# Small tiles padded so that the operands behind them start at multiples of 128 bytes of a partition

## The chip, the core and the metric

The kernel runs on one core of one Trainium2 chip. The metric is the device time of one execution in microseconds (us). Five engines work side by side and are tied by semaphores: TensorE (PE in the profile, its weight loads as PEld), VectorE (DVE), ScalarE (ACT), GpSimd (POOL) and SyncE (SP), which issues the transfers.

## What is computed

A gated linear-attention layer with a running state (mLSTM) for 4 batches, 8 heads, 768 steps and head size 40, followed by a feed-forward layer whose nonlinearity is a quotient of polynomials. `q`, `k`, `v` and the gates come in as 32-bit floats, `w_in` and `w_out` as 64-bit ones, which the kernel splits into a high and a low part.

```python
for t in range(S):                                   # attention, per batch and head
    m_new = max(f[t] + m, i[t])
    C = exp(f[t] + m - m_new) * C + exp(i[t] - m_new) * outer(v[t], k[t]);  m = m_new
    n = (same decay) * n + (same gate) * k[t]
    y[t] = sigmoid(o[t]) * (C @ q[t]) / max(|n . q[t]|, 1)
x = y as [3072 tokens, 320]
h = x @ w_in                                         # [3072, 2048]
g = (a0 + a1 h + a2 h^2 + a3 h^3) / (1 + |b0||h| + |b1|h^2 + 1e-6)
out = g @ w_out                                      # [3072, 320]
```

## The kernel before

The tokens are worked in 12 blocks of 256. A block belongs to two attention units (`attention(u)`, 24 of them: six chunks of 128 steps times four batches), whose outputs are put together by `outputs(m)` and turned into a tile `xk` of [128, 5, 256] that holds x and its remainder in single-precision operands that TensorE reads at its fast rate (`F32R`). `feed_forward(n, i)` then runs eight times per block, each time over 256 of the 2048 inner features:

- `f_f1` makes `ph` (PSUM): 16 matmuls of 256 columns. The moving operand is a slice of `xk`, the stationary one 128 columns of `wi`, `wj` or `wY` (the weights and their remainders).
- ACT, DVE and POOL make g from `ph`, as a high part `gH` and a low part `gL`.
- `f_f2` adds to `po` (PSUM): 12 matmuls of 320 columns. Here the stationary operand is a slice of `gH` or `gL`, and the moving one is `wo`.

So there are 12 x 8 x 16 = 1536 matmuls into `ph` and 12 x 8 x 12 = 1152 into `po`, all `F32R`. The attention's matmuls and transposes (`ps`, `ow`, `y`, `kq`, `px`) are plain `F32`. A plain `F32` product of two operands appears in the profile as two matmuls, a transpose (`kq`, `px`) as one. `hot` are matmuls of `ident` with `ident` that keep TensorE busy while the first inputs arrive.

The order of the instructions on every engine is a list of names written out in the file (`ORDER`); the place of each tile follows from the pools, which lay their tiles one behind the other and begin each at a multiple of 32 bytes of the partition. The pool `common` comes first, with `ident`, `cd` (two numbers), `kp`, `qn0`, `vb0` and `g`; then the constants with the states `st0` to `st5` and `sm0`, `sm1`, the weights, and the working pools with `tm`, `na`, `xk`, `ha`, `w`, `p`, `gH`, `gL` and `ot`. Since `cd` takes 32 bytes and a state 672, nearly everything behind them starts 32, 64 or 96 bytes past a multiple of 128.

```python
c = {name: pool.tile(shape, F32, name=name) for name, shape in (
    ("ident", [P, P]), ("cd", [P, 2]), ("kp", [P, H, L]), ...
st = [cp.tile([DP, NP, E1], F32, name=f"st{j}") for j in range(B + 2)]
```

Of the kernel before, what the change touches and what calls it, by code (L numbers as in the profile page):

```python
# [10 lines left out]
F32 = mybir.dt.float32  # L11
# [298 lines left out]
def kernel(tc: tile.TileContext, *args):  # L310


    with ExitStack() as ctx:
        common = _prologue(ctx, tc, args)
        flag = common.pop("flag")()
        with tc.If(flag > 0) as test:
            _program(tc, True, common, *args)
        with test.Else():
            _program(tc, False, common, *args)


def _prologue(ctx, tc, args):


    nc = tc.nc
    P, L, H, D, BH = 128, 64, 8, 40, 32
    pool = ctx.enter_context(tc.tile_pool(name="common", bufs=1))
    c = {name: pool.tile(shape, F32, name=name) for name, shape in (
        ("ident", [P, P]), ("cd", [P, 2]), ("kp", [P, H, L]), ("qn0", [P, H, L]), ("vb0", [P, H, 2, D + 1]),
        ("g", [P, H * L]),  # L330
    )}
    c["flag"] = _can_square(ctx, tc, args[8])
    for j, src in enumerate((args[4], args[3])):
        nc.sync.dma_start(
            c["g"][0:BH, j * 4 * L : (j + 1) * 4 * L], src.rearrange("b h s -> (b h) s")[:, 0 : 4 * L]
        )
    nc.vector.memset(c["kp"], 0.0)
    nc.vector.memset(c["vb0"], 0.0)
    make_identity(nc, c["ident"])
    nc.gpsimd.memset(c["cd"][:, 0:1], CD)  # L340
    nc.gpsimd.memset(c["qn0"], 0.0)
    return c


def _can_square(ctx, tc, moe_a):

    pool = ctx.enter_context(tc.tile_pool(name="flag", bufs=1))
    a, b = (pool.tile([1, 4], F32, name=f"flag_{x}") for x in "ab")
    t = pool.tile([1, 4], F32, name="flag_t")
    out = pool.tile([1, 1], I32, name="flag_out")  # L350
    tc.nc.sync.dma_start(a, moe_a.unsqueeze(0))

    def decide():
        return _decide(tc, a, b, t, out)

    return decide


def _decide(tc, a, b, t, out):
    V = tc.nc.vector  # L360
    V.scalar_tensor_tensor(b, a, -1.0, a, op0=ALU.mult, op1=ALU.max)
    V.tensor_reduce(t[:, 0:1], b, axis=mybir.AxisListType.X, op=ALU.add)
    V.tensor_scalar(t[:, 1:2], b[:, 3:4], t[:, 0:1], 4.0, op0=ALU.mult, op1=ALU.mult)
    V.scalar_tensor_tensor(t[:, 1:2], a[:, 2:3], a[:, 2:3], t[:, 1:2], op0=ALU.mult, op1=ALU.is_le)
    V.tensor_scalar(t[:, 2:3], t[:, 0:1], 2.0**-20, 1e-30, op0=ALU.mult, op1=ALU.max)
    V.scalar_tensor_tensor(t[:, 2:3], t[:, 2:3], b[:, 3:4], t[:, 1:2], op0=ALU.is_le, op1=ALU.mult)
    V.tensor_copy(out, t[:, 2:3])
    return tc.nc.values_load(out, min_val=0, max_val=1)
# [3 lines left out]
def _program(  # L372
# [17 lines left out]
    B, H, S, D = q.shape  # L390
    DM, DFF = w_in.shape
    P = 128
    L = 64
    NB = S // P
    BH = B * H
    NP = H // 2
    DP = D + L
    E1 = D + 1
# [15 lines left out]
    cp = ctx.enter_context(tc.tile_pool(name="const", bufs=1))  # L414
# [6 lines left out]
    ident, cd = common["ident"], common["cd"]  # L421
# [10 lines left out]
    qn = [common["qn0"], cp.tile([P, H, L], F32, name="qn1")]  # L432
    kp = common["kp"]
    qt = [cp.tile([DP, NP, 2, L], F32, name=f"qT{j}") for j in range(2)]
    vb = [common["vb0"], cp.tile([P, H, 2, E1], F32, name="vb1")]
    st = [cp.tile([DP, NP, E1], F32, name=f"st{j}") for j in range(B + 2)]
    sm = [cp.tile([DP, NP, E1], F32, name=f"sm{j}") for j in range(2)]

    wt = {}
    wY = wp.tile([P, DFF], F32R, name="wY")  # L440
# [1 line left out]
    def ring(pool, tag, shape, name, dt=F32, at=None):  # L442
        k = plan.slot[tag] if at is None else at
        return pool.tile(shape, dt, tag=f"{tag}{k}", name=name, bufs=1)
# [387 lines left out]
    def attention(u):  # L832
        n, b = divmod(u, B)
# [3 lines left out]
        d = units[u] = {}  # L837
# [137 lines left out]
                )  # L975

        def decay(c, src):
            d[c] = ap1.tile([DP, NP, E1], F32, tag=f"tm{c}", name=f"tm{u}_{c}")
            nc.gpsimd.tensor_tensor(
                d[c], src, d["ab"][0:DP, c, :, L - 1 : L].broadcast_to([DP, NP, E1]), op=ALU.mult,  # L980
            )
# [51 lines left out]
        if later:  # L1033
            add("d0", "POOL", 0.7, lambda: decay(0, st[old]), r=[*ST2, "ab"], w=["t0"], new=[("t0", ("tm0", 1))])
        add("ow", "PE", 0.85, f_ow, r=["pm.1", "pm.00", "pm.01", V], w=["ow"], new=new("ow"))
        add("u0", "DVE", 0.66, lambda: update(0, s), r=["t0"] if later else [], w=["ow", *SM])
        add("d1", "POOL", 0.74, lambda: decay(1, s), r=[*SM, "ab"], w=["t1"], new=[("t1", ("tm1", 1))])
        d["i1"] = [f"qA_{u}", *(x[1:] for x in SM), *((x[1:] for x in ST2) if later else ())]
        if u % 2:
# [3 lines left out]
    def outputs(m):  # L1043
        n, b = divmod(2 * m, B)
        pair = [units[2 * m + j] for j in range(2)]
        home, bank = pair[0]["home"], pair[0]["bank"]
        d = {}
# [14 lines left out]
        def ye(k):  # L1062
            return d[k][:, 0 : H * E1].rearrange("p (h c e) -> p h c e", h=4, c=2)
# [12 lines left out]

        def f_ab(k):
            if "na" not in d:
                d["na"] = ring(ap1, "na", [P, 2, H], f"na{m}")
            nc.scalar.activation(d["na"][:, k].rearrange("p (h c) -> p h c", h=4), ye(k)[:, :, :, D], AF.Abs)  # L1080

        def f_rc():
# [56 lines left out]
        na = f"na{m}"  # L1139
        for k in range(2):  # L1140
            add("ab", "ACT", 0.1, lambda k=k: f_ab(k), w=[f"y{k}at{m}", f"{na}.{k}"], new=[(na, ("na", 2))] if k == 0 else ())
# [235 lines left out]
    ap1 = ctx.enter_context(tc.tile_pool(name="att1", bufs=1))  # L1377
# [52 lines left out]
```

## Time and profile before

| | us |
|---|---|
| three runs | 514.69, 515.6, 521.54 (median 515.6) |
| the profiled execution | 514.69 |
| its span, first to last instruction | 512.9 |
| what lies around the span | 1.8 |

The profile shows busy time by engine, the clock that TensorE was granted, a chain of work followed back from the last instruction, and a timeline with the start of every instruction. Matmuls are pipelined: the duration of one is longer than the distance to the next, so what a matmul costs is read from the starts of a row of them, not from their durations.

### The profile page before, as it was taken

The numbers are of one execution on the slowest core, as the hardware profiler recorded it, in microseconds if no ns is written. First come the engines' busy times: TensorE is split into PE (matmuls) and PEld (weight loads), VectorE is DVE, ScalarE is ACT, GpSimd is POOL, SyncE is SP. The second block draws the span as 40 slices with busy tenths as digits, with TensorE's granted clock in tenths as the row PEclk, the third lists the DMA queues.
The fourth block names the chain that finished last, engine by engine and source line by source line (L and its number), as shares of the span: only waits on it lengthen the run. The fifth ranks groups of instructions, "written<-read, shape, count | busy, mean of one in ns | idle before, by whom it ended". The sixth has DMA issues, their size and how long they took to land.

```text
span 512.9 us, 14161 instructions
## 1 busy us (share of the span) xinstructions
PE 483.8 (94%) x5631; PEld 465.4 (91%) x5631; DVE 426.0 (83%) x702; ACT 402.4 (78%) x698; POOL 404.9 (79%) x375
## 2 busy tenths in 40 slices
PE   6898779999999999999999999999999999999991
PEld 6797679989999999999999999999999999999990
DVE  7889789889898988898797987877878787787890
ACT  1887788978798787788887789898778788869960
POOL 3679778989899988878787898868777889776770
PEclk9899899999999999999999999999999999999996
DMA  6998897415244341532422335311240120000001
GB/s 169 213 273 161 192 255 123 72 27 123 54 99 104 92 77 25 138 77 70 81 54 58 83 75 102 89 25 49 45 96 19 34 72 0 8 23 1 27 0 33
DMA packets 119117, 42.53 MB, mean 83 GB/s; under 512 B 103554, under 2 KB 111810, under 8 KB 119042
## 3 DMA queue, kind: packets, MB, share of 16 engines
q1 hardware_dynamic: 118912, 41.37, 37.0%
q8 instruction: 46, 0.75, 0.6%
q14 instruction: 29, 0.24, 0.2%
q10 hardware_dynamic: 130, 0.16, 0.1%
HBM read 36.90 MB, written 4.10 MB: 80 GB/s over the span
## 4 chain that ended last, share of the span: by engine, by line
PE 71%; DVE 9%; ACT 5%; DMA 4%; POOL 4%; issue 3%; SPq 1%; POOLq 0%; DVEq 0%; ACTq 0%
PE ph L34 29%; PE po L34 27%; PE y L34 4%; PE kq L34 3%; PE ow L34 3%; PE ps L34 2%; DMA rawo<-in_moe_w_out_dram 2%; DVE p L34 2%; POOL p L34 2%; DVE w L34 1%; PE px L34 1%; DMA rawi<-in_moe_w_in_dram 1%; DVE gL L34 1%; ACT ph L34 1%; DVE gH L34 1%
## 5 line engine op out<-in xcount | busy, mean ns | idle before, releaser
L34 POOL TENSOR_TENSOR p<-p,w 128x512 f32<-128x512 f32 (+1 forms) x97 | 129.5, 1335 | 56.4 <-DVE w L34 55.1
L34 PE MATMUL ph<-xk,wi 128*128 128x256 f32 x1152 | 167.5, 281 | 0.7 <-DVE pm L34 0.4
L34 PEld LDWEIGHTS ph<-xk,wi 128*128 128x128 f32 x1152 | 150.3, 188 | 1.8 <-ACT lo0i L34 0.6
L34 POOL TENSOR_TENSOR w<-w,ha 128x512 f32<-128x512 f32 (+1 forms) x97 | 129.9, 1343 | 10.7 <-ACT w L34 10.2
L34 PE MATMUL po<-wo,gH 128*128 128x320 f32 x768 | 135.5, 312 | 0.1
L34 PEld LDWEIGHTS po<-wo,gH 128*128 128x128 f32 x768 | 115.4, 188 | 1.3 <-DVE gH L34 0.3
L34 DVE SCALAR_TENSOR_TENSOR w<-w,gH 128x512 f32<-128x512 f32 (+1 forms) x97 | 89.5, 922 | 3.9
L34 ACT ACTIVATE ph<-w,cd 128x512 f32<-128x512 f32 (+1 forms) x97 | 66.5, 686 | 28.8 <-POOL w L34 14.4
L34 DVE SCALAR_TENSOR_TENSOR gL<-p,ps,ph 128x512 fp32r<-128x512 f32 (+1 forms) x97 | 71.0, 733 | 21.0 <-POOL p L34 20.0
L34 DVE SCALAR_TENSOR_TENSOR gH<-p,ps,ph 128x512 fp32r<-128x512 f32 (+1 forms) x97 | 71.2, 734 | 15.9 <-ACT ph L34 14.6
L34 PE MATMUL po<-wo,gL 128*128 128x320 f32 x384 | 79.8, 318 | 4.3 <-DVE gL L34 4.2
L34 ACT ACTIVATE w<-ha,ba 128x512 f32<-128x512 f32 (+1 forms) x97 | 78.4, 811 | 3.0
L34 DVE SCALAR_TENSOR_TENSOR p<-p,ps,ph 128x512 f32<-128x512 f32 (+1 forms) x97 | 70.6, 733 | 10.8 <-ACT p L34 10.6
L34 ACT ACTIVATE ha<-ph 128x512 f32<-128x512 f32 (+1 forms) x97 | 57.2, 592 | 24.4 <-PE ph L34 23.6
L34 ACT ACTIVATE p<-ph,ps 128x512 f32<-128x512 f32 (+1 forms) x97 | 65.5, 676 | 2.1 <-DVE gL L34 1.8
L34 PEld LDWEIGHTS po<-wo,gL 128*128 128x128 f32 x384 | 59.0, 188 | 7.5 <-DVE gL L34 6.5
L34 ACT ACTIVATE ph<-ph 128x512 f32<-128x512 f32 (+1 forms) x97 | 56.1, 579 | 2.1
L34 PE MATMUL ph<-xk,wY 128*128 128x256 f32 x192 | 53.5, 279 | 0.0
L34 PE MATMUL ph<-xk,wj 128*128 128x256 f32 x192 | 53.4, 278 | 0.0
L34 PEld LDWEIGHTS ph<-xk,wj 128*128 128x128 f32 x192 | 36.2, 188 | 0.0
L34 PEld LDWEIGHTS ph<-xk,wY 128*128 128x128 f32 x192 | 36.1, 188 | 0.0
L34 POOL TENSOR_TENSOR qA<-qT,ab 104x512 f32<-104x512 f32 x24 | 32.0, 1334 | 0.0
(128 smaller groups left out, 658.7 us busy)
## 6 DMA issues: line engine op xcount, KB each, us to landing
rawo<-in_moe_w_out_dram SPq DMA_DIRECT2D x8, 640.0 KB
ab<-scrA SPq DMA_DIRECT2D x40, 128.0 KB
rawi<-in_moe_w_in_dram SPq DMA_DIRECT2D x8, 512.0 KB
qn<-in_q_dram SPq DMA_DIRECT2D x24, 160.0 KB
kr<-in_k_dram SPq DMA_DIRECT2D x24, 160.0 KB
og<-in_o_gate_dram SPq DMA_DIRECT2D x48, 80.0 KB
vb<-in_v_dram SPq DMA_DIRECT2D x48, 80.0 KB
out_dram<-ot SPq DMA_DIRECT2D x23, 160.0 KB
```

The source lines that it names most:

```text
L34: made = fn(*args, **kwargs)
```

## The change

No instruction is added, taken away or moved: each engine has the same rows in the same order, 4785 of TensorE, 1468 of DVE, 1395 of ACT and 736 of POOL in the built program, and the same shapes (`padded` makes a longer tile and hands on a view of the old shape). Only the places of the tiles change. `cd` becomes 128 bytes long, `vb0` and `vb1` 2688 (2624 before), each state and decay product 768 (656 before, which took 672), and the normalisers `na` 128 (64 before).

```diff
-        ("ident", [P, P]), ("cd", [P, 2]), ("kp", [P, H, L]), ("qn0", [P, H, L]), ("vb0", [P, H, 2, D + 1]),
+        ("ident", [P, P]), ("cd", [P, 32]), ("kp", [P, H, L]), ("qn0", [P, H, L]), ("vb0", [P, 672]),
         ("g", [P, H * L]),
     )}
+    c["vb0"] = c["vb0"][:, 0 : H * 2 * (D + 1)].rearrange("p (h c e) -> p h c e", h=H, c=2)
...
-    vb = [common["vb0"], cp.tile([P, H, 2, E1], F32, name="vb1")]
-    st = [cp.tile([DP, NP, E1], F32, name=f"st{j}") for j in range(B + 2)]
-    sm = [cp.tile([DP, NP, E1], F32, name=f"sm{j}") for j in range(2)]
+
+    def padded(pool, shape, name, **kw):
+        n = int(np.prod(shape[1:]))
+        t = pool.tile([shape[0], -(-n // 32) * 32], F32, name=name, **kw)[:, 0:n]
+        names = "abc"[: len(shape) - 1]
+        return t.rearrange(f"p ({' '.join(names)}) -> p {' '.join(names)}", **dict(zip(names[1:], shape[2:])))
+
+    vb = [common["vb0"], padded(cp, [P, H, 2, E1], "vb1")]
+    st = [padded(cp, [DP, NP, E1], f"st{j}") for j in range(B + 2)]
+    sm = [padded(cp, [DP, NP, E1], f"sm{j}") for j in range(2)]
...
-            d[c] = ap1.tile([DP, NP, E1], F32, tag=f"tm{c}", name=f"tm{u}_{c}")
+            d[c] = padded(ap1, [DP, NP, E1], f"tm{u}_{c}", tag=f"tm{c}")
...
-                d["na"] = ring(ap1, "na", [P, 2, H], f"na{m}")
+                d["na"] = ring(ap1, "na", [P, 32], f"na{m}")[:, 0 : 2 * H].rearrange("p (k h) -> p k h", k=2)
```

Where the tiles lie, as the two built programs have it (bytes past a multiple of 128; all buffers of a name alike unless listed):

```
tile                              before             after
ident                             0                  0
kp, qn0, vb0                      32                 0
qn1, qT, vb1, ab                  96                 0
st0 .. st5                        32 64 96 0 32 64   0
wi, wj, wY, wo                    32                 0
pm, e, kT, qA, gt, kr             32                 0
xn, fb (its own buffer)           0                  0
g (also the other buffer of fb)   96                 0
xk                                96                 0
ha, w, p, gH, gL, ot              96                 0
pb, ps, ba (2 or 4 numbers each)  0 32 64            32 64 96
```

All slices that the matmuls take of `xk`, `wi`, `wj`, `wY`, `wo`, `gH` and `gL` begin whole multiples of 128 bytes into their tile.

## Rows read from the trace of the kernel before

**Rows 1.** The page: busy time by engine, and granted TensorE clock in 40 slices.

```profile
PE 483.8 (94%) x5631; PEld 465.4 (91%) x5631; DVE 426.0 (83%) x702; ACT 402.4 (78%) x698; POOL 404.9 (79%) x375
...
PEclk9899899999999999999999999999999999999996
```

**Rows 2.** The page: the chain that ended last, by engine and by line.

```profile
PE 71%; DVE 9%; ACT 5%; DMA 4%; POOL 4%; issue 3%; SPq 1%; POOLq 0%; DVEq 0%; ACTq 0%
PE ph L34 29%; PE po L34 27%; PE y L34 4%; PE kq L34 3%; PE ow L34 3%; PE ps L34 2%; DMA rawo<-in_moe_w_out_dram 2%; DVE p L34 2%; POOL p L34 2%; DVE w L34 1%; PE px L34 1%; DMA rawi<-in_moe_w_in_dram 1%; DVE gL L34 1%; ACT ph L34 1%; DVE gH L34 1%
```

**Rows 3.** Windows: busy PE, PEld, DVE, ACT, POOL; clock, DMA share, GB/s.

```profile
125.00:200.00 75.00, 74.87 (x938) 72.16 (x939) 66.37 (x101) 60.07 (x104) 67.70 (x62) 1.00 0.38 81
200.00:300.00 100.00, 99.95 (x1210) 96.86 (x1206) 85.64 (x131) 81.97 (x140) 82.85 (x76) 1.00 0.37 79
300.00:400.00 100.00, 99.79 (x1082) 97.70 (x1081) 82.17 (x127) 82.37 (x141) 80.22 (x73) 1.00 0.28 63
400.00:500.00 100.00, 99.06 (x1000) 96.91 (x999) 83.02 (x127) 82.24 (x144) 76.73 (x68) 1.00 0.06 17
```

**Rows 4.** Timeline of TensorE, 470 to 480 us: start, length, instruction, count.

```profile
473.02 1.33 PE L34 MATMUL po<-wo,gH 128*128 128x320 f32 x8
474.19 0.75 PE L34 MATMUL po<-wo,gL 128*128 128x320 f32 x4
474.77 1.33 PE L34 MATMUL po<-wo,gH 128*128 128x320 f32 x8
475.95 0.74 PE L34 MATMUL po<-wo,gL 128*128 128x320 f32 x4
476.53 0.87 PE L34 MATMUL ph<-xk,wi 128*128 128x256 f32 x6
477.24 0.28 PE L34 MATMUL ph<-xk,wj 128*128 128x256 f32 x1
477.35 0.28 PE L34 MATMUL ph<-xk,wY 128*128 128x256 f32 x1
...
478.26 0.28 PE L34 MATMUL ph<-xk,wY 128*128 128x256 f32 x1
```

**Rows 5.** Timeline of TensorE, 30 to 55 us: two rows of `hot`.

```profile
34.01 4.06 PE L34 MATMUL hot<-ident 128*128 128x128 f32 x34
...
38.72 1.60 PE L34 MATMUL hot<-ident 128*128 128x128 f32 x12
```

**Rows 6.** Timeline of TensorE, 458 to 460.5 us: the transposes of `xn`.

```profile
458.83 0.82 PE L34 MATMUL px<-ident,xn 128*128 128x128 f32 x6
```

**Rows 7.** Instructions on the tile `st`: duration in ns, least/median/most, then first and last start.

```profile
L34 PE MATMUL y<-st,qA x320: 227/227/248, 105.4 to 451.3; 40*64 40x41 f32 x160
L34 DVE TENSOR_TENSOR st<-tm,ow x24: 301/316/326, 34.5 to 456.6; 104x164 f32<-104x164 f32 x24
L34 POOL TENSOR_TENSOR tm<-st,ab x20: 455/467/1383, 76.8 to 449.1; 104x164 f32<-104x164 f32 x20
```

**Rows 8.** Instructions on the tile `ident`, in the same columns.

```profile
L34 PEld LDWEIGHTS hot<-ident x180: 186/192/338, 4.0 to 57.1; 128*128 128x128 f32 x180
...
L34 PEld LDWEIGHTS px<-ident,xn x72: 110/138/230, 55.6 to 459.3; 128*128 128x128 f32 x48, 128*64 128x64 f32 x24
L34 PE MATMUL px<-ident,xn x72: 270/273/421, 55.9 to 459.4; 128*128 128x128 f32 x48, 128*64 128x128 f32 x24
```

**Rows 9.** Instructions on the tile `xk`, in the same columns.

```profile
L34 PEld LDWEIGHTS ph<-xk,wi x1152: 186/188/194, 58.3 to 493.4; 128*128 128x128 f32 x192
```

**Rows 10.** Instructions on the tile `fb`, and on `g`: the scans.

```profile
L34 DVE TENSOR_TENSOR_SCAN e<-fb,eye x14: 1159/1223/2062, 16.3 to 418.6; 128x512 f32<-128x512 f32 x14
...
L34 DVE TENSOR_TENSOR_SCAN e<-g,eye x10: 1210/1266/2145, 86.9 to 427.0; 128x512 f32<-128x512 f32 x10
```

## Prediction

> **What bounds the kernel now.** I read the busy shares first. [...] A busy share alone doesn't make TensorE the bound, so the windows come next: from 125 to 500 us TensorE leaves between 0.05 and 0.94 us of each stretch idle, while DVE is idle for 9 to 18 us and ACT and POOL for more [rows 3]. The chain of work that ended last agrees: 71% of it is TensorE, 29% matmuls into `ph` and 27% into `po`, and no other line has more than 4% [rows 2]. So for three quarters of the span the time is set by how closely one matmul follows another, and a transfer or a slow vector instruction costs only where TensorE waits for it. Before 125 us inputs and weights arrive and TensorE waits here and there; after 500 us a short tail follows the last matmul.
>
> The distance between matmuls is the number to look at. 24 matmuls into `po` start from 473.02 to 476.53 us, so one takes 3.51 / 24 = 146.3 ns [rows 4]. [...] Two rows of `hot` with the same ends, 34 and 12 long, differ by (4.06 - 1.60) / (34 - 12) = 111.8 ns for each one more [rows 5]; six transposes of `xn` last 0.82 us, the last of them 0.273, so the five distances between them are (0.82 - 0.273) / 5 = 109 ns [rows 6, 8]. Both are plain `F32`, where 128 columns take as long as 256 columns do here. Their operands (`ident`, `xn`) are the ones that lie at multiples of 128 bytes already; every operand of the `ph` and `po` matmuls lies 32 or 96 bytes past one. [...]
>
> **The change part by part.** The instructions, shapes, queues and waits are the same, so nothing is priced by count; only what an engine or a transfer pays for the place of its operands can change.
>
> *Attention's small tiles* (`st`, `sm`, `tm`, `vb`, `na`), which are those padded. The six states lie at 32, 64, 96, 0, 32 and 64 bytes past a multiple, so the trace of before holds the experiment: the matmuls that read them take 227 ns in least and median, 248 at most, POOL's product 455 and 467, DVE's sum 301 to 326 [rows 7]. Places differ, durations don't (the most, 1383, is three times the median, far too much for a few bytes of place). Zero, and bounded by the spread of DVE, 25 ns x 44 sums = 1 us, off the chain.
>
> *Elementwise work of the feed-forward.* Of ten scans DVE read from `g`, 96 past a multiple, the least is 1210 ns; of those that read `fb`, ten of them on a multiple and four from PSUM, 1159 [rows 10]. The medians are 1266 and 1223. That is at most 4% of one kind of instruction, with 24 of it; DVE isn't the bound in the steady part, so I take zero. For ACT and POOL there is no row with an aligned operand of that size; 0 to 4% of them, hidden under TensorE either way.
>
> *Weight loads.* The load of 128 columns of `ident`, on the grid, has a median of 192 ns, that of `wi`, 32 past it, 188 [rows 8, 9]. So the load doesn't pay for its place. [...]
>
> *Matmuls into `po`*, 1152 of them. Lower bound of the gain: none. [...]
>
> *Matmuls into `ph`*, 1536. Lower bound none; upper bound from a mean of about 116 ns (half the groups at 113, half at 118, an estimate from [rows 4]) to 109, 7 x 1536 = 10.8 us. I take the small value, 113.5 to 111.8, 1.7 x 1536 = 2.6 us, because the extra of 118 appears and goes away at the same place of the same tiles, so it isn't due to the place.
>
> *Sum.* 9.1 + 2.6 = 11.7 us of TensorE's time, between 0 and 23.1. How much arrives? `ph` and `po` are 1536 x 116 + 1152 x 146.3 = 347 us, and the chain has (0.29 + 0.27) x 512.9 = 287 us of them, 83% [rows 2]; the windows say nearly all, for TensorE has no idle time there [rows 3]. DVE would rise from 86% to under 90% of its stretch, so it doesn't take over. At 90%: 10.5 us. The profiled execution took 514.7 us, 512.9 of span and 1.8 around it; the median of the three runs is 515.6. 514.7 - 10.5 = 504.2, say 504.
>
> [...]
>
> **The rivals.**
>
> *The place doesn't matter; the time stays.* [...] Time: 515, within 513 to 518. [...]
>
> [...]
>
> *Slower: the two operands now meet.* Before, weights and moving operand of a matmul lie 64 bytes apart modulo 128 (32 and 96); after, both lie at 0, and the load of the next weights runs while the moving operand is read. `hot`, whose two operands are even the same tile, takes 111.8 ns against 109 of the transposes. If that is the price of meeting, 2.8 ns x 2688 = 7.5 us, 90% of it 6.8: 521.5. It decides the sign when it is more than what alignment gives back; it takes 4.3 ns for each matmul to be slower by 2%. Against it: the transposes have both operands at 0 as well and pay nothing.
>
> *TensorE gets faster, the time hardly.* Then DVE or POOL, 80 to 86% busy in the stretches, with waits between them that the average hides, keep matmuls into `po` waiting for `gL`. Of 11.7 us a third would arrive: 511.
>
> **How the numbers follow.** Forecast, faster matmuls, 0.48, at 504 and from 496 (the upper bound of 23.1 us at 83% is 495.5) to 508. No effect, 0.36, at 515. Gain lost on the way, 0.08, at 511. Slower, 0.08, at 521.5. The range from 496 to 518 leaves out the slower case and the best corner of the forecast. A measurement of this kernel tells from no change about 2%, 10.3 us: the three runs of before are 1.3% apart. Below 505.3 lie some two thirds of the forecast's weight: 0.34. Over 526 half of the slower case: 0.04. The rest, 0.62, is within 2%.
>
> **What would show it.** In the profile of after, at the same stretch of TensorE's timeline, 24 matmuls into `po` in 3.32 us instead of 3.51, and eight into `ph` in 0.89 instead of 0.91. If both stay, the place doesn't matter. [...] If both fall and the time doesn't, look for waits of `po` for `gL`; longer distances on both speak for operands that meet. I'm wrong altogether if the gain sits in the transfers of the first 125 us or in DVE and ACT, whose durations should stay as they are.

## The result and the profile after

The changed kernel is slower by a little: 518.84 us against 515.44, medians of 20 runs each, a ratio of 1.0059 [1.0037, 1.0081]. The forecast of 504 was wrong in sign, and 518.84 lies outside its range of 496 to 518.

TensorE's timeline of the changed kernel, at the stretch that answers to [rows 4] (start, length, instruction, count):

```profile
478.87 0.88 PE L34 MATMUL ph<-xk,wi 128*128 128x256 f32 x6
479.58 0.28 PE L34 MATMUL ph<-xk,wj 128*128 128x256 f32 x1
479.70 0.28 PE L34 MATMUL ph<-xk,wY 128*128 128x256 f32 x1
...
480.66 0.28 PE L34 MATMUL ph<-xk,wY 128*128 128x256 f32 x1
480.78 1.34 PE L34 MATMUL po<-wo,gH 128*128 128x320 f32 x8
481.96 0.75 PE L34 MATMUL po<-wo,gL 128*128 128x320 f32 x4
482.55 1.34 PE L34 MATMUL po<-wo,gH 128*128 128x320 f32 x8
483.72 0.75 PE L34 MATMUL po<-wo,gL 128*128 128x320 f32 x4
484.31 0.88 PE L34 MATMUL ph<-xk,wi 128*128 128x256 f32 x6
```

Into `po` nothing moved: 24 matmuls in 484.31 - 480.78 = 3.53 us, 147 ns each, 146.3 before. Into `ph` eight take 480.66 - 479.70 = 0.96 us, 120 ns, where they took 113.8. Over the whole trace (all distances under 160 ns from one matmul to the next into the same target, from 75 us on; 1362 and 1368 of them for `ph`) the means are 116.1 before and 119.7 after for `ph`, 146.7 and 146.8 for `po`. On the page the same shows as 6.5 us more of busy time for TensorE (483.8 before, [rows 1]) and 6.6 more for its weight loads; of the other engines DVE moved most, by 3.4:

```profile
PE 490.3 (94%) x5631; PEld 472.0 (91%) x5631; DVE 429.4 (82%) x702; ACT 402.0 (77%) x698; POOL 403.7 (78%) x375
...
L34 PE MATMUL ph<-xk,wi 128*128 128x256 f32 x1152 | 172.9, 287 | 0.3 <-DVE xn L34 0.3
L34 PEld LDWEIGHTS ph<-xk,wi 128*128 128x128 f32 x1152 | 155.1, 193 | 1.2 <-ACT lo0i L34 0.6
L34 PE MATMUL po<-wo,gH 128*128 128x320 f32 x768 | 135.8, 313 | 0.0
```

And TensorE is without idle time in the same windows (columns as in [rows 3]):

```profile
125.00:200.00 75.00, 74.92 (x916) 72.44 (x916) 65.80 (x99) 60.34 (x104) 67.17 (x61) 1.00 0.41 85
200.00:300.00 100.00, 100.00 (x1183) 97.13 (x1181) 85.84 (x131) 80.52 (x138) 80.54 (x75) 1.00 0.34 75
```

Where does the time go? One landmark can be followed through all kernels: the ACT instruction that first reads a finished `ph` (`ha`), 97 of them. From the 17th to the last it takes 138.82 to 494.10 us before, 355.3 us, and 142.81 to 502.32 after, 359.5. This **steady stretch** is 4.2 us longer, and the 1264 matmuls into `ph` that start in it have 1264 x 3.5 ns = 4.4 us more. Nearly all of it arrives. What is ahead of the stretch differs by 4.0 us in these two profiled executions, but it differs by as much between executions that should be alike (below), and the medians differ by 3.4 us in all.

### The profile page after: what moved, and what is told of

It reads as the page before. It is cut to its first block, busy times and chain, and to the rows that moved or that the text cites. A ratio compares the mean times of both kernels' runs of the same rounds, so it can differ in the third digit from the quotient of the medians.

```text
span 520.8 us, 14161 instructions
## 1 busy us (share of the span) xinstructions
PE 490.3 (94%) x5631; PEld 472.0 (91%) x5631; DVE 429.4 (82%) x702; ACT 402.0 (77%) x698; POOL 403.7 (78%) x375
## 4 chain that ended last, share of the span: by engine, by line
PE 75%; DVE 7%; DMA 5%; POOL 4%; ACT 2%; issue 2%; SPq 2%; POOLq 0%; DVEq 0%; ACTq 0%
PE ph L34 33%; PE po L34 29%; PE y L34 4%; PE kq L34 3%; DMA rawi<-in_moe_w_in_dram 3%; PE ow L34 3%; PE ps L34 3%; PE px L34 2%; SPq L34 2%; POOL p L34 2%; DMA rawo<-in_moe_w_out_dram 1%; DVE p L34 1%; DVE e L34 1%; DVE w L34 1%; DVE gL L34 1%
## 5 line engine op out<-in xcount | busy, mean ns | idle before, releaser
L34 PE MATMUL ph<-xk,wi 128*128 128x256 f32 x1152 | 172.9, 287 | 0.3 <-DVE xn L34 0.3
L34 PEld LDWEIGHTS ph<-xk,wi 128*128 128x128 f32 x1152 | 155.1, 193 | 1.2 <-ACT lo0i L34 0.6
L34 DVE SCALAR_TENSOR_TENSOR w<-w,gH 128x512 f32<-128x512 f32 (+1 forms) x97 | 88.2, 910 | 3.9
L34 PE MATMUL ph<-xk,wj 128*128 128x256 f32 x192 | 54.6, 285 | 0.0
```

The costliest lines, as they stand in the source:

```text
L34: made = fn(*args, **kwargs)
```

## The experiments

All distances are in bytes modulo 128, place of `xk` less place of the weights, unless 256 is said. Before the change it is 64 (192 modulo 256), after it 0. "`ph` 117.6 ns" is the mean distance between starts, as above; it and the stretch come from one profiled execution of each kernel. The ratio is the time over that of the kernel before, with its 95% interval in brackets.

### Moving xk alone, and moving everything

`xk64` and `bxk64` put an unused tile of 64 bytes ahead of `xk` and one behind it, so that, modulo 128, only `xk` moves; `all32` makes `cd` longer.

```diff
# xk64 (changed kernel) and bxk64 (kernel before)
     xp = ctx.enter_context(tc.tile_pool(name="xk", bufs=1))
+    xp.tile([P, 16], F32, name="xpad")
     fp = ctx.enter_context(tc.tile_pool(name="ffn", bufs=2))
+    fp.tile([P, 16], F32, name="fpad", bufs=1)
# all32 (changed kernel)
-        ("ident", [P, P]), ("cd", [P, 32]),
+        ("ident", [P, P]), ("cd", [P, 40]),
```

> The changed kernel with the four xk tiles alone moved on by 64 bytes, so that xk lies at 64 and the weights at 0 of 128: 64 apart, as before the change, but at other places. Theory 1, the two operands of a matmul into ph cost when they lie at the same place modulo 128: ph falls from a mean of 119.7 ns between starts to about 116 (113 to 118), the time to 514 to 516. Theory 2, each operand's own place counts, and 0 is a bad one for the weights: ph stays at 120, the time near 519. Theory 3, it is the other engines' tiles, all on the grid now: ph stays at 120. po stays at 146.7 in all three.

Measured: `ph` 117.6 ns, the stretch 357.2 us, ratio 1.0028 [0.9999, 1.0058]. It falls, by two of the 3.5 ns and not the whole way to the 116 of theory 1. Theories 2 and 3 had it stay.

> The kernel before with the four xk tiles alone moved on by 64 bytes: xk at 32, where the weights are, everything else where it was. Theory 1: ph rises from 116.1 to about 120 ns, the time by 3 to 6 us to 518 to 521. Theory 2 for the weights' place and theory 3: ph stays at 116, the time at 515; theory 2 for the place of xk: either, with no reason for 120 in particular.

Measured: `ph` 119.6 ns, the stretch 359.1 us, ratio 1.0072 [1.0040, 1.0104]. Moving four tiles by 64 bytes in the kernel before makes all of the change's loss, with no tile on the grid that wasn't. Its timeline has eight in 482.95 - 481.99 = 0.96 us, as the changed kernel's:

```profile
481.99 0.28 PE L34 MATMUL ph<-xk,wY 128*128 128x256 f32 x1
482.11 0.88 PE L34 MATMUL ph<-xk,wi 128*128 128x256 f32 x6
482.83 0.28 PE L34 MATMUL ph<-xk,wj 128*128 128x256 f32 x1
482.95 0.28 PE L34 MATMUL ph<-xk,wY 128*128 128x256 f32 x1
```

> The changed kernel with every tile from kp on moved by 32 bytes (cd 160 bytes long), so that both operands lie at 32: off the grid, but together. Theory 1: as the changed kernel, ph near 120 ns, about 519 us. Theory 2, place by itself: ph changes, to 113 to 118 if 32 is good for the weights, or to more if being off the grid costs. Theory 3 (all engines' tiles on multiples of 128): ph back to 116, 515 us.

Measured: `ph` 119.6 ns, the stretch 359.4 us, ratio 1.0055 [1.0028, 1.0082]. Off the grid but together is as bad as on it together. The place by itself (theory 2) and the other engines' tiles (theory 3) fall with these three. Nor is it how far `xk` lies from the tiles behind it, `ha` to `gL`: in the built programs that is 0 in the kernel before (116.1 ns) as in the changed kernel (119.7), and 64 in `xk64` (117.6) as in `bxk64` (119.6).

### Which padding did it

`rest` takes the padding of `tm` and `na` back out of the changed kernel, and `tmna` puts it alone into the kernel before. Both tiles lie between the weights and `xk`, and their padding adds 320 bytes there, 64 modulo 128; the other padded tiles lie ahead of the weights and move both operands alike.

```diff
# rest (changed kernel; tmna is the reverse, in the kernel before)
-            d[c] = padded(ap1, [DP, NP, E1], f"tm{u}_{c}", tag=f"tm{c}")
+            d[c] = ap1.tile([DP, NP, E1], F32, tag=f"tm{c}", name=f"tm{u}_{c}")
...
-                d["na"] = ring(ap1, "na", [P, 32], f"na{m}")[:, 0 : 2 * H].rearrange("p (k h) -> p k h", k=2)
+                d["na"] = ring(ap1, "na", [P, 2, H], f"na{m}")
```

> The changed kernel without the padding of the decay products tm and the normalisers na, the rest of the change kept. Weights and states stay on the grid, and xk comes to lie 64 past it (192 of 256), as far from the weights as before the change. Theory 1 (the operands' distance): ph back to 116 ns between starts, 515 us, within 0.3% of before; the padding of cd, vb, st and sm does nothing by itself. Theory 2 (the grid itself costs): ph stays at 119 to 120, 518 to 519 us.

Measured: `ph` 116.4 ns, the stretch 355.8 us, ratio 1.0017 [0.9994, 1.0039]: as before the change, though weights and states are on the grid. Its timeline shows 113 ns where the kernel before does, 479.88 to 480.78 for eight:

```profile
478.97 0.28 PE L34 MATMUL ph<-xk,wY 128*128 128x256 f32 x1
479.08 0.84 PE L34 MATMUL ph<-xk,wi 128*128 128x256 f32 x6
479.76 0.28 PE L34 MATMUL ph<-xk,wj 128*128 128x256 f32 x1
479.88 0.28 PE L34 MATMUL ph<-xk,wY 128*128 128x256 f32 x1
...
480.78 0.28 PE L34 MATMUL ph<-xk,wY 128*128 128x256 f32 x1
```

> The kernel before with the padding of tm and na alone: everything ahead of them stays, off the grid, and xk comes to lie at 32, where the weights are. Theory 1: ph 119.6 ns, ratio to before near 1.006, all of the change's loss from two small tiles that no matmul into ph reads. Theory 2: ph 116, ratio 1.000.

Measured: `ph` 119.7 ns, the stretch 359.4 us, ratio 1.0096 [1.0068, 1.0125]. The load of the weights shows it too, with medians of 192 ns here and 188 in `rest`; of `tmna`, then of `rest`, the view of the tile `xk` (duration least/median/most, first and last start):

```profile
L34 PEld LDWEIGHTS ph<-xk,wi x1152: 186/192/333, 58.3 to 498.8; 128*128 128x128 f32 x192
L34 PE MATMUL ph<-xk,wi x1152: 277/283/580, 58.3 to 498.9; 128*128 128x256 f32 x192
```

```profile
L34 PEld LDWEIGHTS ph<-xk,wi x1152: 186/188/333, 56.5 to 495.1; 128*128 128x128 f32 x192
L34 PE MATMUL ph<-xk,wi x1152: 276/281/583, 56.5 to 495.2; 128*128 128x256 f32 x192
```

Padding `tm` and `na`, which no matmul into `ph` touches, is the whole loss. The ratio is larger than the changed kernel's though the steady stretch is the same; where the rest comes from, no run shows.

### A map of distances

`dose` makes every weight tile but `wY` 32 bytes longer, so that each begins 32 bytes further on; `x1` and `x2` put unused tiles of 32 to 192 bytes ahead of each of the four `xk`, and one behind them.

```diff
# dose (changed kernel; the last tile takes 224 bytes)
-            t = wp.tile([P, n, 2], I32, tag=name, name=raw)
+            t = wp.tile([P, 2 * n + SLACK.get(name, 8)], I32, tag=name, name=raw)[:, 0 : 2 * n]
+            t = t.rearrange("p (n w) -> p n w", w=2)
...
# x1: XPAD = {0: 96, 1: 64, 2: 128, 3: 96};  x2: XPAD = {0: 192, 1: 32, 2: 96, 3: 128}
         k = plan.slot[tag] if at is None else at
+        if tag == "xk" and XPAD.get(k):
+            pool.tile([P, XPAD.pop(k) // 4], F32, name=f"xpad{k}", bufs=1)
...
```

> The changed kernel with each weight tile 32 bytes further on than the one before, so that in one run wi and wo lie at 0, 32, 64 and 96 of 128, and xk, gH and gL at 0. Theory 1: ph by the distance of wi from xk: 120 at 0 (wi6), and 113 to 118 at 64 (wi1), with 32 and 96 between or like one of the two. Theory 2: some order that follows the place of wi alone, which this run can't part from theory 1, but xk64 can. Theory 3: one value for all. For po theory 1 has no forecast, as 64 and 0 apart gave the same 146.7; if place matters at all for po, the wo tiles at 32 and 96 show another value than that.

Measured: `ph` 118.0 ns in the mean, by the place of the weights that are loaded next 118.6 at 0, 118.4 at 32, 117.5 at 64 and 117.5 at 96; 357.6 us for the stretch, 517.07 in one run. The order is right and the steps are small. Eight matmuls in a row take weights from three tiles at different places, so neighbours may blur each other; no run separates them. `po` has 146.5 to 147.3 for `wo` at 0, 32 and 64 (none lies at 96): it hardly reacts.

> The changed kernel with its four xk tiles at different places, weights at 0: two that serve one block each at 96 and 160 of 256, the two that serve five each at 32 and 128. Theory 1 with period 128: 120 ns for the one at 128, less for 32, 96 and 160. With period 256: less at 128 too. If one place gives a steady 113 ns, a layout faster than both kernels by up to 2.8 ns x 1536 = 4.3 us is there.

Measured: 117.1 ns with `xk` at 32, 119.8 at 96, 118.0 at 160, 118.7 at 128. The last is near the 119.7 of distance 0, as with a period of 128, though 1 ns short of it. No steady 113. The tile at 96 is a miss of theory 1: it had less than 120 there. The same places again show that the pair counts: `xk` at 96 is slow here, with the weights at 0, and not in the kernel before, with them at 32 (116.1); `xk` at 32 is slow in `bxk64`, with them at 32 (119.6), and less so here.

> As x1, with xk at 192 and 224 of 256 for one block each, and 64 and 192 for five each. The kernel before had the distance 192 and a mean of 116.1, xk64 the distance 64 and 117.6. If that difference is one of place, the tile at 192 shows 116 and that at 64 shows 117.6; if it is chance (the state in which a run of matmuls begins), both show the same, 116 to 118.

Measured: 114.7 and 115.6 ns for the two tiles at 192, 116.0 for that at 64, 118.2 at 224. So 64 of 128 is the best distance of those tried, and 0 the worst together with 96. The latter rests on one block each in `x1` (119.8) and `x2` (118.2) and on `dose`, where weights at 32 are a distance of 96 (118.4) and weights at 96 one of 32 (117.5). To lie at the same place is thus not the whole rule. That the tile at 64 shows 116.0 here and all four showed 117.6 in `xk64` is not explained by the place; both values come from the same two levels, 113 and 118 ns, in other shares. The steady stretches are 357.5 us for `x1` and 355.3 for `x2`, the latter as in the kernel before; the whole times, 522.12 and 520.44 in one run each, are longer mainly because both reach the first `ha` 5.6 to 5.8 us later, at 66.8 and 66.9 us against 61.1.

### Why ph and not po

Both have both operands at 0 after the change. `po` was cut to 256 columns in the changed kernel and in `rest`, then `ph` to 192 in the same two. Both leave out part of the products.

```diff
# po256_0, po256_64
+                    if f:
+                        hi = lo + 256
                     po = PO[n][b][:, at : at + hi - lo]
# ph192_0, ph192_64
-                    nc.tensor.matmul(to, w, x[:, kx], start=(o == 0), stop=(o == 7))
+                    e = T if o == 0 else 192
+                    nc.tensor.matmul(to[:, 0:e], w, x[:, kx, 0:e], start=(o == 0), stop=(o == 7), skip_group_check=True)
```

> The changed kernel (moving and stationary operands both at 0) with the matmuls into po cut to 256 of their 320 columns, except those of the first inner feature block; the last 64 output columns so miss most of their sum. Why did po not react to place? Theory 1a: because its 320 columns are longer than the load of the next 128 weights, which has the length of 256 columns; cut to 256 it behaves as ph: 119 to 120 ns at distance 0. Theory 1b: place doesn't matter to po for another reason (its weights change every second matmul, its products go to two banks in turn): then 113 to 118 here, the same as in its twin.

Measured: `po` 121.3 ns in the mean, 120 the commonest; without the uncut matmuls, which still take about 147, the mean is 119.5. The starts, eight in 470.95 - 469.99 = 0.96 us:

```profile
469.99 1.12 PE L34 MATMUL po<-wo,gH 128*128 128x256 f32 x8
470.95 0.64 PE L34 MATMUL po<-wo,gL 128*128 128x256 f32 x4
```

> The same cut in the kernel without the padding of tm and na, where gH and gL lie 64 from wo and xk 64 from the weights. Theory 1a: po at 113 to 118 ns, 2 to 6 less than in the twin at distance 0, as ph (116 against 120). Theory 1b: the same as the twin.

Measured: `po` 118.6 ns in the mean, 2.6 less than its twin, with 118 and 117 commonest and 113 and 114 for one in six; without the uncut ones 116.8. Eight in 478.77 - 477.83 = 0.94 us:

```profile
477.83 1.10 PE L34 MATMUL po<-wo,gH 128*128 128x256 f32 x8
478.77 0.85 PE L34 MATMUL ph<-xk,wi 128*128 128x256 f32 x6
```

`po` cut to 256 columns behaves as `ph` does (119.5 and 116.8 against 119.7 and 116.4), as theory 1a forecast; how long the load is, which it gives as the reason, these two don't show.

> The changed kernel with the matmuls into ph cut to 192 of 256 columns, except the first of each eight; a quarter of the tokens so miss most of the product. [...]

> The same cut in the kernel without the padding of tm and na, xk 64 from the weights. If the cost of the same place is paid by the load, it is there too with a short stream: 3 to 6 ns less here than in the twin. If it is paid by the stream, the load hides it: the same in both.

Measured: 110.8 ns at distance 0 and 111.4 at 64 (the means hold one full matmul in eight; the cut ones alone have 108.3 and 108.5). Eight in 0.90 us in both, `ph192_0` and then `ph192_64`:

```profile
475.95 0.27 PE L34 MATMUL ph<-xk,wY 128*128 128x192 f32 x1
...
476.85 0.28 PE L34 MATMUL ph<-xk,wY 128*128 128x192 f32 x1
```

```profile
475.48 0.28 PE L34 MATMUL ph<-xk,wY 128*128 128x192 f32 x1
...
476.38 0.27 PE L34 MATMUL ph<-xk,wY 128*128 128x192 f32 x1
```

With 64 columns fewer `ph` falls to 111, not to the 88 that 192 columns would take at the 146.8 / 320 = 0.46 ns a column of `po`, an estimate. What remains, 0.90 / 8 = 112.5 ns in the rows above at either distance, I read as the load of the next weights; no run times the load by itself. And there the place doesn't matter, as it doesn't with 320 columns (146.7 ns at 64 before the change, 146.8 at 0 after it). So of the three lengths tried the loss appears only at 256 columns, where by the same estimate the stream takes 117 ns, about as long as what remains.

That distance counts is shown, by moving `xk` alone and the weights alone. That load and stream get into each other's way in what they read is an explanation that fits these lengths; no run shows it, nor what they would share, nor why a distance of 96 costs about as much as 0. Equal place is not enough either: `hot` reads one tile for both, 128 columns in plain `F32`, and takes 111.8 ns [rows 5], less than the 113.8 of eight matmuls into `ph` [rows 4]. The loss is shown for `F32R` alone.

### How much of a gain arrives

The same four runs answer a second question. From the changed kernel to `po256_0`, 965 matmuls into `po` that start in the stretch have 25.5 ns less in the mean, 24.6 us; the stretch falls from 359.5 to 352.0 us, 7.5 us. From `rest` to `po256_64` it is 28 ns, 27 us, and 355.8 falls to 352.4, 3.4 us. Both end at 352, and so do the kernels with `ph` cut, at 352.6 and 352.8, although `ph192_64` has only 5.0 ns x 1264 = 6.3 us less than `rest`. Of `po256_64`, 125 to 500 us, who waited (in all, times, longest, us):

```profile
PE po L34 <- DVE gL L34: 9.5, 17, 1.1
PE po L34 <- DVE gH L34: 1.8, 3, 0.7
```

The same list of the kernel before:

```profile
PE po L34 <- DVE gL L34: 1.2, 4, 0.5
```

The list counts only time in which TensorE is shown idle. The starts show more: distances of over 160 ns from one matmul to the next add up to 26.3 us of the stretch in `rest`, 116 of them, and to 55.4 us in `po256_64`, 190 of them. Less a usual 0.12 us for each of the 74 more, that is some 20 us, most of the 23.6 that did not arrive. So the time taken from TensorE comes back as waits, by the list above all for DVE's products. Some 3 us below the kernel before something else than TensorE sets the pace; that it is the loop through ACT, POOL and DVE, in these queues' written order, is the likely reading, and no run moves that order.

## Why the prediction was wrong

- **The bound, right above and wrong below.** "TensorE leaves between 0.05 and 0.94 us of each stretch idle" is so, and a loss of 4.4 us arrived as 4.2. But I read the windows as if a gain would arrive as well, "at 90%". Matmuls are shown 276 to 308 ns long and start 113 to 147 ns apart, so a wait of some 150 ns leaves no idle time on the page. A cut of 27 us brought 3.4, some 13%. Even with the places as I thought, 11.7 us would have brought about 3, an estimate from the four cut kernels, which all end there.
- **Small tiles, zero:** right. `rest` has them all on the grid but two, and is as fast as before within 0.4%.
- **Weight loads:** "the load doesn't pay for its place" was read from `hot`, 192 ns, and `wi`, 188. The reading compared place with place, where with 256 columns the distance decides: 192 in every kernel with distance 0, the cut `po` of `po256_0` included, 188 in `rest` and `xk64`. But 192 by itself is no sign of a shared place: `ph192_64` has it at a distance of 64, and `po` with 320 columns has 188 at 0. So what the 192 of `hot` comes from stays open.
- **Matmuls into po, 9.1 us of the sum, 8 ns of each:** the term that carried the forecast was my estimate, and it failed. No run shows it, nor the 23.1 us at the upper end: 24 of them took 3.53 us, not 3.32, and the mean is 146.3 to 146.9 ns in every kernel with 320 columns, at all the places tried.
- **Matmuls into ph, 1.7 ns less:** 3.5 more. That they could come down to the 111.8 of `hot`, the 2.6 us of the sum, no run with 256 columns shows: the lowest mean of a tile is 114.7, in `x2`. The extra of 118 over 113 "isn't due to the place": it isn't due to the place of one tile; that a distance of 64 has the two levels mixed and 0 has mostly one, at 120, is due to two.
- **The rivals.** The slower one was the mechanism: "the two operands now meet", priced at 2.8 ns and 2688 matmuls, 6.8 us. It is 3.5 ns, and 1536 of them, 5.4 us in all. The price came near by luck: the 2.8 ns were read from `hot`, which goes about as fast as `ph192` at either distance (111.8 ns against 110.8 and 111.4). I gave it 0.08 because the transposes have both operands at 0 and pay nothing; but their load is shown shorter than that of `hot` (138 ns against 192, [rows 8]), and with 192 and 320 columns, in `ph192` (110.8 ns at 0 and 111.4 at 64) and in `po` (146.8 and 146.7), nothing is paid either. The 0.62 for a time within 2% came true for a reason that had 0.08, not for the one that had 0.36. Single places change nothing that the runs show: both operands moved on by 32 bytes, their distance kept, have 119.6 ns in `all32` where there were 119.7.

## What to carry to other kernels

A tile's place counts in pairs: for `F32R` matmuls of 256 columns with new weights each, 64 bytes modulo 128 between stationary and moving operand was the best distance tried, here worth 3.5 ns of 120. Check that distance after any padding between them. Read what a gain would bring by taking work out of the engine that seems to bound, in one run, before building it: here TensorE was busy 99.6% from 125 to 500 us [rows 3] and had 3 us to give.

## What was not expected

Padding of two tiles that TensorE never reads beside `ph` cost 0.6 to 1%, by moving what lies behind them. Two levels, 113 and 118 ns, hold for most groups of eight and often for several groups in a row, at the same tiles; what sets them is open. So is the part ahead of the first `ha`, which took 59.8 to 66.9 us in the fourteen profiles with the same instructions in it, more than the whole effect.
